# First loads in order of use on two queues, and k and q in turn, in a fused linear-attention and GEGLU kernel

## The chip, the cores and the metric

The kernel runs on one core of a Trainium2 chip. The time is device microseconds of one execution. Each kernel was timed in several executions. All runs below were classed as "fast". The profile is of one of those executions, and its span is about 1.4 us shorter than the time of the same run.

Names used below: PE is the tensor engine, PEld its weight loads, DVE the vector engine, ACT the scalar engine, SP the engine that here only issues transfers. A *pair* is the two matmuls, 512 and 128 columns wide, with which one 128-row block of x meets one 128-row piece of a weight matrix. Five pairs make k (or q) of one tile of 128 tokens.

## The reference, cut to what matters

```python
# S = 2048 tokens, D = 640, 32 heads of 20, F = 1728, bf16
qkv = x @ wqkv                                   # q, k, v
pq, pk = phi(q), phi(k)                          # phi(t) = (t + 1 if t > 0 else exp(t)) + 1e-6
kv, z = einsum(pk, v), pk.sum(tokens)
a = (einsum(pq, kv) / (einsum(pq, z) + 1e-6)) @ wo
b = (gelu(x @ w_gate) * (x @ w_up)) @ w_down
g = sigmoid((x * gate_w).sum(-1))
out = g * a + (1 - g) * b
```

The change touches only how the kernel gets started: the first loads, and the stage that computes phi(k) and phi(q) for the 16 tiles of x.

## The kernel before

A helper records every operation with the data that it reads and writes, and derives the semaphore waits from that. Each engine runs its operations in the order in which they were recorded (PE in before: `T(0)` at 3.36 us, `T(1)` at 4.65, the first pair at 5.05, `T(2)` at 5.54). The first three tiles of x (0, 1, 2) are loaded plainly and transposed on PE; the other 13 come through transposing transfers. `wk` and `wq` are the k and q columns of `wqkv`, five pieces of 128 rows each (160 KB a piece).

```python
dma_in(gw_sb[0:5, :], gate_w..., [r_gw], eng="act")
for k in range(KC):                                              # KC = 5
    dma_in(wk[:, k, :], A_wqkv[k*128:(k+1)*128, 640:1280], [r_wk[k]], eng="act")
for i in range(NXN):                                             # NXN = 3
    dma_in(x_aug[:, i, 0:640], A_x[0, i*128:(i+1)*128, :], [r_xn[i]])        # on SP
for i in range(NXN, NT):                                         # NT = 16
    load_xT(i)                                                   # transposing, on SP
# ... later loads cut ...

def T(i):        # five 128x128 transposes on PE into one bank, one DVE copy to xT
def KM(i, ks):   # pairs of k of tile i for the pieces ks of wk, into the two banks of slot(i)
def QM(i):       # five pairs of q of tile i (one more column: the gate)
def phi1(n):     # ACT: exp of the slot
def phi2(n):     # DVE: min, then max(t + 1, ...): frees the slot's banks

warm(6, 512)     # matmuls on constants, meant to get PE's clock up (e11 runs without them)
T(0); warm(2, 128); T(1); warm(2, 128)
KM(0, [0]); T(2)
# ... transpose of the gate column, its copy into wq ...
KM(1, [0])
for k in range(1, KC):
    KM(0, [k]); KM(1, [k]); KM(2, [k - 1])
KM(2, [KC - 1])
for n in range(2 * NT):          # 16 tiles of k, then 16 of q
    if n >= NT: QM(n - NT)
    elif n >= 3: KM(n, list(range(KC)))
    phi1(n); phi2(n)
    if n == 3: dma_in(wq[:, :, 0:640], ..., [r_wq], eng="act")
# ... pk^T x, FFN with geglu, normalisation, output: unchanged, cut ...
```

There are four slots of two PSUM banks each. The pairs of tile 4 go to the slot of tile 0, so they wait until DVE has finished phi of tile 0 (12.60 us in before, where they start at 12.66).

## Time and profile before

| | value | where it is read |
|---|---|---|
| time | 277.33 us, median of the first 3 runs | runs |
| span of the profiled run | 275.9 us | page |
| PE busy | 98% | page, part 1 |
| chain of waits on PE | 95% | page, part 4 |
| PE idle before the fourth piece of wk | 1.27 us | timeline |
| k of tile 3 starts / k of tile 4 starts | 11.29 / 12.66 us | timeline |

The page of before, part 1 (engine, busy us and share, number of instructions):

```profile
span 275.9 us, 4037 instructions
...
PE 269.3 (98%) x1663; PEld 139.6 (51%) x1696; DVE 138.4 (50%) x233; ACT 78.2 (28%) x132; POOL 26.0 (9%) x28
```

The timeline of before, PE only (start, duration, engine, line, operation, output and input, shape, count; in brackets the idle time just before and what ended it). L386 is the warm-up, L402 the transposes of a tile, L418 the 512-wide half of a k pair:

```profile
0.84 2.72 PE L386 MATMUL ps<-const-bfloat16-1.0 128*128 128x512 bf16 x6 [0.84 <-PEq L790]
...
3.36 0.63 PE L402 MATMUL ps<-pool 128*128 128x128 bf16 x5
...
4.65 0.45 PE L402 MATMUL ps<-pool 128*128 128x128 bf16 x5 [0.55 <-DMA pool<-in_A_x_dram]
...
5.05 0.38 PE L418 MATMUL ps<-pool 128*128 128x512 bf16 x1
...
9.38 0.39 PE L418 MATMUL ps<-pool 128*128 128x512 bf16 x1 [1.27 <-DMA pool<-in_A_wqkv_dram]
...
11.29 0.38 PE L418 MATMUL ps<-pool 128*128 128x512 bf16 x1
...
12.66 0.39 PE L418 MATMUL ps<-pool 128*128 128x512 bf16 x1
```

One sees the first transposes at 3.36 us, as soon as x tile 0 is there, the first pair at 5.05, and eight pairs later the only long idle time. A duration of 0.38 us is not the cost of a matmul: pairs follow each other every 0.27 us, and their records overlap (the first 512-wide one lasts from 5.05 to 5.43 us, the next matmul starts at 5.27). From 11.29 us on PE is dense.

What the idle PE waited for is in the view of transfers, taken over a stretch that two issues share (2.80 to 2.90 us): destination and source, queue, kind, count, KB, and us from issue to landing.

```profile
pool<-in_A_wqkv_dram ACTq DMA_DIRECT2D x1, 160.0 KB, 6.6
pool<-in_A_x_dram SPq DMA_TRANSPOSE x1, 7.6
```

The fourth piece of wk, issued at 2.75 us, landed 6.6 us later, while x tile 0, issued at 0.81, had needed 2.3. In the stretch from 5 to 6 us the same view shows why one may suspect the transposing loads (packets, bytes, rate, packets by size; then the ACT queue's own share):

```profile
DMA packets 469, 0.24 MB, mean 244 GB/s; under 512 B 343, under 2 KB 469, under 8 KB 469
...
q10 hardware_dynamic: 145, 0.16, 62.5%
```

Most packets (343 of 469) are the small ones of the transposes by then, and the rate has fallen, from 353 GB/s in the microsecond before to 244, although at least three pieces of wk are still under way on the ACT queue (q10).

### The profile page before, as it was taken

The numbers are of one execution on the slowest core, as the hardware profiler recorded it, in microseconds if no ns is written. First come the engines' busy times: TensorE is split into PE (matmuls) and PEld (weight loads), VectorE is DVE, ScalarE is ACT, GpSimd is POOL, SyncE is SP. The second block draws the span as 40 slices with busy tenths as digits, with TensorE's granted clock in tenths as the row PEclk, the third lists the DMA queues.
The fourth block names the chain that finished last, engine by engine and source line by source line (L and its number), as shares of the span: only waits on it lengthen the run. The fifth ranks groups of instructions, "written<-read, shape, count | busy, mean of one in ns | idle before, by whom it ended". The sixth has DMA issues, their size and how long they took to land.

```text
span 275.9 us, 4037 instructions
## 1 busy us (share of the span) xinstructions
PE 269.3 (98%) x1663; PEld 139.6 (51%) x1696; DVE 138.4 (50%) x233; ACT 78.2 (28%) x132; POOL 26.0 (9%) x28
## 2 busy tenths in 40 slices
PE   7899999999999999999999999999999999999997
PEld 4455555555545444444444444444555555555553
DVE  2398888610244224999999999535100122212223
ACT  1355555310432354222322223224555100000000
POOL 5000000000000400332423322000000000000000
PEclk9999999999999999999999999999999999999999
DMA  7999997002030112122121221390000011111111
GB/s 183 165 200 251 397 399 234 12 0 50 14 57 11 47 52 61 24 48 40 33 49 24 48 41 32 56 314 14 0 0 2 9 43 46 48 50 48 50 39 56
DMA packets 36400, 22.38 MB, mean 81 GB/s; under 512 B 25759, under 2 KB 34975, under 8 KB 36383
## 3 DMA queue, kind: packets, MB, share of 16 engines
q1 hardware_dynamic: 34997, 20.49, 27.6%
q10 hardware_dynamic: 1386, 1.64, 2.3%
q8 instruction: 13, 0.21, 0.4%
q14 instruction: 4, 0.03, 0.0%
HBM read 13.11 MB, written 2.62 MB: 57 GB/s over the span
## 4 chain that ended last, share of the span: by engine, by line
PE 95%; DMA 2%; issue 1%; ACTq 1%; DVE 0%
PE ps L595 41%; PE ps L738 20%; PE ps L431 6%; PE ps L701 6%; PE ps L502 6%; PE ps L418 5%; DMA pool<-in_A_wqkv_dram 2%; PE ps L504 2%; PE ps L432 2%; PE ps L702 2%; PE ps L419 2%; PE ps L570 2%; PE ps L722 1%; ACTq L330 1%; PE ps L616 1%
## 5 line engine op out<-in xcount | busy, mean ns | idle before, releaser
L595 PE MATMUL ps<-pool 128*128 128x512 bf16 x509 | 113.0, 379 | 0.6
L595 PEld LDWEIGHTS ps<-pool 128*128 128x128 bf16 x520 | 50.4, 98 | 60.0 <-issue 0.3
L738 PE MATMUL ps<-pool 128*128 128x128 bf16 (+1 forms) x407 | 56.6, 297 | 0.6 <-issue 0.2
L603 DVE TENSOR_TENSOR pool<-ps,pool 128x512 bf16<-128x512 f32 x52 | 35.7, 687 | 33.6 <-PE ps L595 30.4
L601 ACT ACTIVATE pool<-ps 128x512 f32<-128x512 f32 x52 | 31.0, 597 | 72.5 <-PE ps L595 72.1
L749 DVE SCALAR_TENSOR_TENSOR pool<-ps,pool 128x512 bf16<-128x512 f32 (+1 forms) x32 | 16.2, 547 | 63.8 <-PE ps L738 63.8
L738 PEld LDWEIGHTS ps<-pool 128*128 128x128 bf16 x416 | 31.8, 98 | 25.3 <-issue 1.1
L647 POOL TENSOR_TENSOR pool<-pool 128x640 f32<-128x640 bf16 x16 | 22.4, 1404 | 140.5 <-DMA pool<-z_row 87.4
L440 ACT ACTIVATE pool<-ps 128x640 bf16<-128x640 f32 x32 | 22.3, 703 | 23.4 <-PE ps L419 13.8
L453 DVE SCALAR_TENSOR_TENSOR pool<-ps,pool 128x640 bf16<-128x640 f32 x32 | 26.4, 824 | 2.2
L655 DVE TENSOR_TENSOR pool<-pool 128x640 bf16<-128x640 bf16 x16 | 23.0, 1440 | 0.6
L418 PE MATMUL ps<-pool 128*128 128x512 bf16 x77 | 21.6, 379 | 1.3 <-DMA pool<-in_A_wqkv_dram 1.3
L431 PE MATMUL ps<-pool 128*128 128x512 bf16 x77 | 21.4, 379 | 0.0
L701 PE MATMUL ps<-pool 128*128 128x512 bf16 x77 | 21.3, 379 | 0.0
L502 PE MATMUL ps<-pool 128*128 128x512 bf16 x76 | 21.2, 379 | 0.0
L504 PE MATMUL ps<-pool 128*128 128x129 bf16 x80 | 17.6, 220 | 0.2
L432 PE MATMUL ps<-pool 128*128 128x129 bf16 x80 | 17.6, 220 | 0.2
L702 PE MATMUL ps<-pool 128*128 128x128 bf16 x80 | 17.5, 219 | 0.2
L419 PE MATMUL ps<-pool 128*128 128x128 bf16 x80 | 17.5, 219 | 0.2
L706 ACT ACTIVATE pool<-ps,pool 128x640 f32<-128x640 f32 x16 | 12.7, 793 | 9.2 <-PE ps L702 9.2
L450 DVE TENSOR_SCALAR pool<-pool 128x640 bf16<-128x640 bf16 x32 | 10.4, 325 | 7.9 <-ACT pool L440 6.3
L418 PEld LDWEIGHTS ps<-pool 128*128 128x128 bf16 x80 | 7.8, 98 | 10.8 <-DMA pool<-in_A_wqkv_dram 1.6
(51 smaller groups left out, 128.9 us busy)
## 6 DMA issues: line engine op xcount, KB each, us to landing
out_dram<-pool SPq DMA_DIRECT2D x15, 160.0 KB, 1.8
pool<-in_B_w_gate_dram SPq DMA_DIRECT2D x1, 2080.0 KB, 13.9
pool<-in_B_w_up_dram SPq DMA_DIRECT2D x1, 2080.0 KB, 18.5
pool<-in_A_x_dram SPq DMA_DIRECT2D x1, 1280.0 KB, 7.7
pool<-in_B_w_down_dram SPq DMA_DIRECT2D x1, 1120.0 KB, 6.0
pool<-in_A_wo_dram SPq DMA_DIRECT2D x6, 160.0 KB, 8.8
pool<-in_B_w_down_dram SPq DMA_DIRECT2D x1, 960.0 KB, 8.4
pool<-in_A_wqkv_dram ACTq DMA_DIRECT2D x5, 160.0 KB, 4.4
```

The costliest lines, as they stand in the source:

```text
L418: e.matmul(ps[:, b0, :], lhs, wk[:, k, 0:512], start=(k == 0), stop=(k == KC - 1))
L419: last = e.matmul(ps[:, b1, 0:128], lhs, wk[:, k, 512:640], start=(k == 0), stop=(k == KC - 1))
L431: e.matmul(ps[:, b0, :], lhs, wq[:, k, 0:512], start=(k == 0), stop=(k == KC - 1))
L432: last = e.matmul(ps[:, b1, 0:129], lhs, wq[:, k, 512:641], start=(k == 0), stop=(k == KC - 1))
L453: P.op("dve", lambda e: e.scalar_tensor_tensor(dst, ps_flat[:, b0 * 512:b0 * 512 + 640], 1.0 + EPS, e_buf[m], ALU.add, ALU.max), reads=[ba ...
L502: e.matmul(ps[:, bs[n], :], lhs, x_aug[:, i, 0:512], start=(i == 0), stop=(i == NT - 1))
L504: last = e.matmul(ps[:, bt, n * 129:(n + 1) * 129], lhs, x_aug[:, i, 512:641], start=(i == 0 and n == 0), stop=(i == NT - 1), skip_group_c ...
L595: last = e.matmul(ps[:, b, :], w[:, k, fc * 128:(fc + 1) * 128], xT[:, k, j * 512:(j + 1) * 512], start=(k == 0), stop=(k == KC - 1))
L601: P.op("act", lambda e: e.activation(ge[n], ps[:, gb, :], ACT.Gelu_apprx_tanh), reads=[bank[gb]], writes=[r_ge[n]])
L603: P.op("dve", lambda e: e.tensor_tensor(hT[fc][:, j * 512:(j + 1) * 512], ps[:, ub, :], ge[n], ALU.mult), reads=[bank[ub], r_ge[n]], write ...
L701: e.matmul(ps[:, b0, :], lhs, w2[:, m, 0:512], start=(m == 0), stop=(m == KC - 1))
L738: last = e.matmul(dst, lhs, wd[:, fc, c0:c0 + cn], start=False, stop=(fc == NFC - 2), skip_group_check=True)
```

## The change

The intent: the first loads in the order of their use, spread over both queues (x0, wk1, x2, wk3 on SP; wk0, x1, wk2, wk4 on ACT); the transposing loads not before wk1 has landed; wq moved from ACT into the stream of transposing loads; k of seven tiles first, then q and k in turn, so that later transposed tiles are needed at half the pace; and tile 0's first block transposed and copied alone, so that the first pair can start early.

```diff
+KLEAD = 7
-dma_in(gw_sb[0:5, :], gate_w..., [r_gw], eng="act")
-for k in range(KC):
-    dma_in(wk[:, k, :], ..., [r_wk[k]], eng="act")
-for i in range(NXN):
-    dma_in(x_aug[:, i, 0:640], ..., [r_xn[i]])
+load_x(0, "sp");  load_wk(0, "act")
+load_wk(1, "sp"); load_x(1, "act")
+load_x(2, "sp");  load_wk(2, "act")
+load_wk(3, "sp"); load_wk(4, "act")
+dma_in(gw_sb[0:5, :], gate_w..., [r_gw], eng="act")
 for i in range(NXN, NT):
-    load_xT(i)
+    if i == KLEAD:
+        dma_in(wq[:, :, 0:640], ..., r_wq)
+    load_xT(i, after=([r_wk[1]] if i == NXN else ()))
 ...
+seq = [("k", i) for i in range(KLEAD)] + [("q", 0)]
+for i in range(KLEAD, NT):
+    seq += [("q", i - KLEAD + 1), ("k", i)]
+seq += [("q", i) for i in range(NT - KLEAD + 1, NT)]
 ...
 warm(6, 512)
-T(0); warm(2, 128); T(1); warm(2, 128); KM(0, [0]); T(2); <gate column>; KM(1, [0])
-for k in range(1, KC):
-    KM(0, [k]); KM(1, [k]); KM(2, [k - 1])
-KM(2, [KC - 1])
+T(0, [0], 7); T(0, [1, 2, 3, 4], 6)
+KM(0, [0]); T(1, [0, 1, 2, 3, 4], 7); KM(0, [1]); warm(2, 128)
+KM(1, [0]); KM(1, [1]); T(2, [0, 1, 2, 3, 4], 6)
+KM(0, [2]); KM(1, [2]); KM(2, [0]); KM(2, [1]); KM(2, [2]); gate_col()
+for k in range(3, KC):
+    for n in range(3):
+        KM(n, [k])
```

(Cut: bookkeeping of which data a step reads, and `phi1`, `phi2`, `QM` looking up their tile in `seq`.)

More of the change, by code (lines that the diff above doesn't have):

```diff
@@ L299, in bass_gated_mix__linear_attn_block__geglu_ffn__prompt_kernel @@
             r_xT = [P.sb("xT%d" % i, R_XT, R_XT + KC * S) for i in range(NT)]
+            r_x0a = P.sb("x0a", R_XT, R_XT + 128)
             r_wk = [P.sb("wk%d" % k, R_WK + k * 640, R_WK + (k + 1) * 640) for k in range(KC)]
-            r_wq = P.sb("wq", R_WQ, R_WQ + KC * XW)
+            r_wq = [P.sb("wq%d" % k, R_WQ + k * XW, R_WQ + k * XW + 640) for k in range(KC)]
             r_gcol = P.sb("gcol", R_WQ, R_WQ + KC * XW)
@@ L331, in dma_in, with load_x, load_wk @@
                      reads=reads, writes=writes, dma=new_dma_key())
+            def load_x(i, eng):
+                dma_in(x_aug[:, i, 0:640], A_x[0, i * 128:(i + 1) * 128, :], [r_xn[i]], eng=eng)
+            def load_wk(k, eng):
+                dma_in(wk[:, k, :], A_wqkv[k * 128:(k + 1) * 128, 640:1280], [r_wk[k]], eng=eng)
+            load_x(0, "sp")
+            load_wk(0, "act")
+            load_wk(1, "sp")
+            load_x(1, "act")
+            load_x(2, "sp")
+            load_wk(2, "act")
+            load_wk(3, "sp")
+            load_wk(4, "act")
             dma_in(gw_sb[0:5, :], gate_w.rearrange("(k p) -> k p", p=128), [r_gw], eng="act")
-            for k in range(KC):
-                dma_in(wk[:, k, :], A_wqkv[k * 128:(k + 1) * 128, 640:1280], [r_wk[k]], eng="act")
-            for i in range(NXN):
-                dma_in(x_aug[:, i, 0:640], A_x[0, i * 128:(i + 1) * 128, :], [r_xn[i]])
             def load_xT(i, after=()):
@@ L345, in bass_gated_mix__linear_attn_block__geglu_ffn__prompt_kernel @@
             for i in range(NXN, NT):
-                load_xT(i)
+                if i == KLEAD:
+                    dma_in(wq[:, :, 0:640], A_wqkv[:, 0:640].rearrange("(k p) w -> p k w", p=128), r_wq)
+                load_xT(i, after=([r_wk[1]] if i == NXN else ()))
             dma_in(x_aug[:, NXN:8, 0:640],
@@ L394, in slot, with T @@
                 return SLOTS[n] if n < 3 else SLOTS[n % 4]
-            def T(i):
-                tb = 6 + i % 2
+            def T(i, ks, tb):
                 def fn(e):
                     last = None
-                    for k in range(KC):
-                        last = e.transpose(psb[:, tb, k * 128:(k + 1) * 128],
+                    for n, k in enumerate(ks):
+                        last = e.transpose(psb[:, tb, n * 128:(n + 1) * 128],
                                            x_aug[:, i, k * 128:(k + 1) * 128], ident)
@@ L406, in T, with KM @@
                 P.op("dve", lambda e: e.tensor_copy(
-                    xT[:, :, i * 128:(i + 1) * 128],
-                    psb[:, tb, 0:640].rearrange("p (k s) -> p k s", k=KC)),
-                    reads=[bank[tb]], writes=[r_xT[i]])
-            def KM(i, ks):
-                b0, b1 = slot(i)
+                    xT[:, ks[0]:ks[-1] + 1, i * 128:(i + 1) * 128],
+                    psb[:, tb, 0:len(ks) * 128].rearrange("p (k s) -> p k s", k=len(ks))),
+                    reads=[bank[tb]], writes=[r_x0a if i == 0 and ks[0] == 0 else r_xT[i]])
+            seq = [("k", i) for i in range(KLEAD)] + [("q", 0)]
+            for i in range(KLEAD, NT):
+                seq += [("q", i - KLEAD + 1), ("k", i)]
+            seq += [("q", i) for i in range(NT - KLEAD + 1, NT)]
+            def KM(n, ks):
+                i = seq[n][1]
+                b0, b1 = slot(n)
                 def fn(e):
@@ L421, in fn, with QM @@
                     return last
-                P.op("pe", fn, reads=[r_xT[i]] + [r_wk[k] for k in ks], writes=[bank[b0], bank[b1]])
-            def QM(i):
-                b0, b1 = slot(NT + i)
+                P.op("pe", fn, reads=[r_x0a if i == 0 and ks == [0] else r_xT[i]] + [r_wk[k] for k in ks],
+                     writes=[bank[b0], bank[b1]])
+            def QM(n):
+                i = seq[n][1]
+                b0, b1 = slot(n)
                 def fn(e):
@@ L434, in fn @@
                     return last
-                P.op("pe", fn, reads=[r_xT[i], r_wq, r_gcol], writes=[bank[b0], bank[b1]])
+                P.op("pe", fn, reads=[r_xT[i], r_gcol] + r_wq, writes=[bank[b0], bank[b1]])
             def phi1(n):
@@ L441, in phi1 @@
                      reads=[bank[b0], bank[b1]], writes=[r_e[m]])
-                if n >= NT:
-                    i = n - NT
+                kind, i = seq[n]
+                if kind == "q":
                     P.op("act", lambda e: e.activation(eg[:, i:i + 1], ps[:, b1, 128:129], ACT.Tanh, scale=0.5),
@@ L451, in phi2 @@
                      reads=[r_e[m]], writes=[r_e[m]])
-                dst, r_dst = (pk[n], r_pk[n]) if n < NT else (pq[n - NT], r_pq[n - NT])
+                kind, i = seq[n]
+                dst, r_dst = (pk[i], r_pk[i]) if kind == "k" else (pq[i], r_pq[i])
                 P.op("dve", lambda e: e.scalar_tensor_tensor(
@@ L455, in phi2, with gate_col @@
                     reads=[bank[b0], bank[b1], r_e[m]], writes=[r_dst])
-            warm(6, 512)
-            T(0)
-            warm(2, 128)
-            T(1)
-            warm(2, 128)
-            KM(0, [0])
-            T(2)
-            P.op("pe", lambda e: e.transpose(psb[:, 7, 0:5], gw_sb[0:5, :], ident[0:5, 0:5]),
-                 reads=[r_gw, r_ident], writes=[bank[7]])
-            P.op("dve", lambda e: e.tensor_copy(wq[:, :, 640:641],
-                                                psb[:, 7, 0:5].rearrange("p (k o) -> p k o", o=1)),
-                 reads=[bank[7]], writes=[r_gcol])
-            KM(1, [0])
-            for k in range(1, KC):
-                KM(0, [k])
-                KM(1, [k])
-                KM(2, [k - 1])
-            KM(2, [KC - 1])
+            def gate_col():
+                P.op("pe", lambda e: e.transpose(psb[:, 7, 0:5], gw_sb[0:5, :], ident[0:5, 0:5]),
+                     reads=[r_gw, r_ident], writes=[bank[7]])
+                P.op("dve", lambda e: e.tensor_copy(wq[:, :, 640:641],
+                                                    psb[:, 7, 0:5].rearrange("p (k o) -> p k o", o=1)),
+                     reads=[bank[7]], writes=[r_gcol])
+            warm(6, 512)
+            T(0, [0], 7)
+            T(0, [1, 2, 3, 4], 6)
+            KM(0, [0])
+            T(1, [0, 1, 2, 3, 4], 7)
+            KM(0, [1])
+            warm(2, 128)
+            KM(1, [0])
+            KM(1, [1])
+            T(2, [0, 1, 2, 3, 4], 6)
+            KM(0, [2])
+            KM(1, [2])
+            KM(2, [0])
+            KM(2, [1])
+            KM(2, [2])
+            gate_col()
+            for k in range(3, KC):
+                for n in range(3):
+                    KM(n, [k])
             for n in range(2 * NT):
-                if n >= NT:
-                    QM(n - NT)
+                if seq[n][0] == "q":
+                    QM(n)
                 elif n >= 3:
@@ L481, in bass_gated_mix__linear_attn_block__geglu_ffn__prompt_kernel @@
                 phi2(n)
-                if n == 3:
-                    dma_in(wq[:, :, 0:640], A_wqkv[:, 0:640].rearrange("(k p) w -> p k w", p=128), [r_wq],
-                           eng="act")
                 if n == 6:
```

## The prediction

> **What bounds the kernel.** The tensor engine. The page of before shows PE busy 98% of a 275.9 us span, and the chain of waits is 95% PE. The table of stretches shows PE busy 9.9 of 10 us from 12 us to the end of the k/q stage, granted clock 1.0 throughout. So nothing after about 12 us can be shortened by this change: it moves loads and reorders the same 32 k/q tiles, which cost 5 pairs of matmuls at 0.27 us, 1.36 us each. ACT (0.70 us) and DVE (0.33 + 0.82 us) per tile stay below that. Only the start can be won.
>
> **The start in the timeline.** x tile 0 lands at 3.1 us; the first k pair starts at 5.05 after five transposes, a 0.49 us copy and small warm-up matmuls, with 0.55 us of PE idle. Eight pairs have run by 8.11, then PE idles 1.27 us, until 9.38, for the fourth piece of wk, which was issued at 2.75 and landed 6.6 us later, sharing the DMA engines with thirteen transposing x loads that were issued from 2.2 us on. The seven remaining pairs end at 11.28, where k of tile 3 starts. The same work packed from first data is about 4.1 us of pairs plus 1 us of transposes.
>
> **What the change does.**
> 1. x0 and wk0 go first on two queues, then wk1/x1, x2/wk2, wk3/wk4; transposing loads wait until wk1 has landed. Eight loads of 160 KB are 1.31 MB. With both queues plain the trace moved about 300 to 350 GB/s (3 to 5 us), so I estimate 1 us per couple: landings near 3.3, 4.3, 5.3 and 6.3 us. [...] I credit the gain to order and to the transposes kept out, not to added bandwidth. Issues here cost 0.37 to 0.45 us.
> 2. Tile 0's first block is transposed and copied alone: the first pair at about 3.9 instead of 5.05 us.
> 3. From these: T2 done near 6.1, seven pairs by 7.5, gate column, last eight pairs without a stall, k of tile 3 near 9.2 instead of 11.28. Gain 2.1 us.
> 4. Costs: transposing loads begin near 4.4 instead of 2.2 us. Alone they landed 3.0 to 4.0 us after issue, one every 1.28 us: tile 3 near 8.2, tile 6 near 12.5, each before its use (9.2, 13.4). wq sits between tiles 6 and 7: issued near 9.5, landing (5.5 us before, beside transposes) 14 to 15 us, against first use near 14.8. This is the tight spot; up to 0.7 us may be lost.
> 5. After that k and q alternate, so each transposed tile is needed every 2.7 us, and their supply has slack. No work is added later; the stages after k/q should only shift.
>
> **Prediction.** 275.3 us (0.993), range 274.4 to 276.6. Faster by over 2% would need 5.5 us, more than the whole startup idle: chance 0.01. Within 2%: 0.98. Slower: 0.01.
>
> **What would show it.** Timeline: first k pair near 3.9 us, no wait of PE on wk over 0.3 us, tile 3's k near 9.2; wait of q0 on wq under 0.7 us; PE busy total the same within 1 us; later stages starting about 2 us earlier with equal lengths.
>
> **What would make it wrong.** x0 arriving later because wk0 shares its engines (each 0.3 us costs as much); wk3/wk4 caught by the transposes again; tile 3 or wq late, which would hand the gain back at once, since PE has no slack afterwards.

That the second queue would add no bandwidth was the assumption (measured afterwards, from 2 to 3 us: 201 GB/s from one queue in before, 207 from two in the changed kernel). The forecast's sum: landings 1 us apart, the first pair at 3.9, k of tile 3 at 9.2, a gain of 2.1 us.

## The result, and the profile after

| | before | after |
|---|---|---|
| time, median of 6 runs (lowest to highest) | 277.39 us (277.02 to 277.52) | 276.73 us (276.53 to 278.38) |
| ratio | | 0.9988, 95% interval 0.9964 to 1.0012 |
| span of the profiled run | 275.9 us | 275.2 us |
| first transposes start | 3.36 us | 4.17 us |
| first pair starts | 5.05 us | 4.72 us |
| k of tile 3 starts | 11.29 us | 10.36 us |
| k of tile 4 starts | 12.66 us | 12.00 us |
| span minus start of tile 4 | 263.2 us | 263.2 us |

A ratio is the mean time of one kernel's fast runs over that of the other's fast runs of the same rounds, so it is not quite the ratio of the medians. Here one run of 278.38 us among five of 276.5 to 277.0 pulls the mean up. The interval contains 1, so these runs alone do not show that the changed kernel is faster; what follows reads two profiles, and the experiments below bear it out.

The last row says where the whole difference between the two profiles lies: after k of tile 4 has started, both take the same 263.2 us. The second half of the change, k and q in turn, moved nothing; all of their difference, 12.66 - 12.00 = 0.66 us, was won in the first 12 us. Forecast had been 2.1 us.

The page after, part 1. (The higher busy time than before is not work: records of matmuls are missing from the trace of before, which has 1663 for 1696 weight loads, against 1694 for 1694 after.)

```profile
span 275.2 us, 4067 instructions
...
PE 271.3 (99%) x1694; PEld 139.3 (51%) x1694; DVE 138.8 (50%) x234; ACT 78.3 (28%) x132; POOL 26.1 (9%) x28
```

The timeline after, PE, the lines that answer to those of before (L401 warm-up, L415 transposes, L438 k pair):

```profile
0.84 2.72 PE L401 MATMUL ps<-const-bfloat16-1.0 128*128 128x512 bf16 x6 [0.84 <-PEq L818]
4.17 0.45 PE L415 MATMUL ps<-pool 128*128 128x128 bf16 x5 [0.61 <-DMA pool<-in_A_x_dram]
4.72 0.39 PE L438 MATMUL ps<-pool 128*128 128x512 bf16 x1
...
6.04 0.39 PE L438 MATMUL ps<-pool 128*128 128x512 bf16 x1 [0.20 <-DVE pool L419]
...
10.36 0.38 PE L438 MATMUL ps<-pool 128*128 128x512 bf16 x1
...
12.00 0.39 PE L438 MATMUL ps<-pool 128*128 128x512 bf16 x1
```

The long idle time before 9.38 us is gone, as intended. But the first transposes now start 0.81 us later than before, the second tile's first pair waits for a copy (L419), and tile 4, which needs 1.36 us after tile 3 when nothing is in the way, starts 1.64 us after it.

The transfers after: the two first loads (issued at 0.80 and 0.81 us), in the columns used above.

```profile
pool<-in_A_wqkv_dram ACTq DMA_DIRECT2D x1, 160.0 KB, 3.1
pool<-in_A_x_dram SPq DMA_DIRECT2D x1, 160.0 KB, 3.3
```

x0 needed 3.3 us instead of 2.3. (In the other profiles whose two first loads are these it needed 2.9 to 3.3 us, so a single landing time has a scatter of about 0.4 us.) wk0 landed at 3.9 us; in before, where it was issued at 1.40, at 4.8. And the stretch from 5 to 6 us, which is now plain packets (48 of 303 are under 512 B, where before had 343 of 469):

```profile
DMA packets 303, 0.33 MB, mean 328 GB/s; under 512 B 48, under 2 KB 303, under 8 KB 303
...
q10 hardware_dynamic: 141, 0.15, 42.1%
```

The chain of waits after, in order of time (start, us, what), shows the links of the start:

```profile
0.81 3.32 DMA pool<-in_A_x_dram
4.17 0.24 PE ps L415
4.44 0.24 DVE pool L419
4.72 0.39 PE ps L438
...
5.49 0.50 DVE pool L419
6.04 0.39 PE ps L438
...
10.02 0.71 ACT pool L462
10.75 0.34 DVE pool L472
11.12 0.84 DVE pool L476
12.00 0.39 PE ps L438
```

The last four lines are phi of tile 0: its exp starts only at 10.02, when its last pair has ended, and its bank is free at 12.00. That is the 0.28 us between tiles 3 and 4.

### The profile page after: what moved, and what is told of

Same layout as the page of the kernel before. It is cut to its first block, busy times and chain, and to the rows that moved or that the text cites. A ratio compares the mean times of both kernels' runs of the same rounds, so it can differ in the third digit from the quotient of the medians.

```text
span 275.2 us, 4067 instructions
## 1 busy us (share of the span) xinstructions
PE 271.3 (99%) x1694; PEld 139.3 (51%) x1694; DVE 138.8 (50%) x234; ACT 78.3 (28%) x132; POOL 26.1 (9%) x28
## 4 chain that ended last, share of the span: by engine, by line
PE 96%; DMA 1%; DVE 1%; ACT 0%; issue 0%
PE ps L623 41%; PE ps L766 20%; PE ps L530 6%; PE ps L729 6%; PE ps L453 6%; PE ps L438 6%; PE ps L454 2%; PE ps L532 2%; PE ps L730 2%; PE ps L598 2%; PE ps L439 1%; DMA pool<-in_A_x_dram 1%; PE ps L750 1%; PE ps L644 1%; PE ps L660 1%; DVE pool L777 0%
## 5 line engine op out<-in xcount | busy, mean ns | idle before, releaser
L623 PE MATMUL ps<-pool 128*128 128x512 bf16 x520 | 113.7, 379 | 0.0
L766 PE MATMUL ps<-pool 128*128 128x512 bf16 (+1 forms) x416 | 57.2, 299 | 0.0
L438 PE MATMUL ps<-pool 128*128 128x512 bf16 x80 | 23.5, 380 | 0.5 <-DVE pool L419 0.2
L453 PE MATMUL ps<-pool 128*128 128x512 bf16 x80 | 22.9, 379 | 0.0
L530 PE MATMUL ps<-pool 128*128 128x512 bf16 x80 | 21.9, 379 | 0.0
L729 PE MATMUL ps<-pool 128*128 128x512 bf16 x80 | 21.8, 379 | 0.0
L677 DVE TENSOR_REDUCE pool<-pool 128x32 f32<-128x640 f32 x16 | 13.0, 810 | 0.0
L438 PEld LDWEIGHTS ps<-pool 128*128 128x128 bf16 x80 | 7.8, 98 | 10.1 <-DVE pool L419 1.0
```

Source lines behind the costliest of these rows:

```text
L438: e.matmul(ps[:, b0, :], lhs, wk[:, k, 0:512], start=(k == 0), stop=(k == KC - 1))
L453: e.matmul(ps[:, b0, :], lhs, wq[:, k, 0:512], start=(k == 0), stop=(k == KC - 1))
L530: e.matmul(ps[:, bs[n], :], lhs, x_aug[:, i, 0:512], start=(i == 0), stop=(i == NT - 1))
L623: last = e.matmul(ps[:, b, :], w[:, k, fc * 128:(fc + 1) * 128], xT[:, k, j * 512:(j + 1) * 512], start=(k == 0), stop=(k == KC - 1))
L729: e.matmul(ps[:, b0, :], lhs, w2[:, m, 0:512], start=(m == 0), stop=(m == KC - 1))
L766: last = e.matmul(dst, lhs, wd[:, fc, c0:c0 + cn], start=False, stop=(fc == NFC - 2), skip_group_check=True)
```

## The experiments

Theory: the whole difference, and the whole shortfall, lies before k of tile 4. Of the 2.1 us, 0.8 went to x0, which shares the DMA engines with wk0 now (from 3 to 4 us the packets of SP's queue took 48.6% of the 16 engines' time, those of ACT's 61.5%); the rest to copies that PE waits for and to the order of the pairs. Rivals: k and q in turn gives something back (e1); the hold of the transposing loads costs or gains (e2); x0 was late for another reason (e3). While these ran, PE's clock came up as another rival, which the later runs test. Every kernel gave the correct result. Ratios are against the kernel before, which ran beside each group (medians 277.35 to 277.57 us; in the group of e9 to e12 its runs went from 276.54 to 279.56, which widens those intervals: the kernel before has an occasional slow run too). By the verdict at 2% every kernel of the table counts as "same"; differences of a few tenths of a microsecond are read from intervals, from groups of runs and from profiles.

| kernel | median us (lowest to highest) | ratio, 95% interval |
|---|---|---|
| e1 all k, then all q | 276.71 (276.35 to 276.98) | 0.9980 (0.9968 to 0.9993) |
| e2 no hold | 276.49 (276.39 to 277.07) | 0.9977 (0.9964 to 0.9990) |
| e3 x0 alone first | 277.20 (277.13 to 278.26) | 1.0010 (0.9993 to 1.0028) |
| e4 tile 0's pairs first | 276.36 (276.28 to 276.50) | 0.9968 (0.9956 to 0.9981) |
| e5 seven warm-ups | 276.65 (276.40 to 277.06) | 0.9978 (0.9965 to 0.9992) |
| e6 = e4 + seven warm-ups | 276.26 (275.92 to 276.56) | 0.9962 (0.9948 to 0.9975) |
| e7 = e4, x0 and wk0 in halves | 278.74 (278.00 to 279.72) | 1.0054 (1.0035 to 1.0074) |
| e8 before, new loads only | 279.70 (276.71 to 280.33) | 1.0061 (1.0019 to 1.0103) |
| e9 = e6 without hold | 276.34 (276.10 to 276.56) | 0.9956 (0.9925 to 0.9986) |
| e10 = e8, idle gaps filled | 276.74 (276.42 to 277.17) | 0.9974 (0.9945 to 1.0002) |
| e11 no warm-up | 277.90 (277.44 to 278.36) | 1.0014 (0.9985 to 1.0042) |
| e12 tile 0 transposed whole | 278.28 (276.97 to 278.55) | 1.0015 (0.9982 to 1.0047) |
| e13 = e7, idle gaps filled | 277.29 (277.06 to 279.03) | 1.0011 (0.9986 to 1.0035) |
| e14 = e12, idle gap filled | 277.14 (276.75 to 277.60) | 0.9995 (0.9974 to 1.0015) |

### e1: the alternation undone

```diff
-seq = [("k", i) for i in range(KLEAD)] + [("q", 0)] ...
+seq = [("k", i) for i in range(NT)] + [("q", i) for i in range(NT)]
```

> The changed kernel, with the alternation of k and q undone (all k, then all q); loads and prologue kept. Theory S (the whole difference to before, and the whole shortfall, lies in the first 12 us): the same time as the changed kernel, 276.7 us within 0.2, as PE is dense after 12 us there and each transposed tile still lands before its use. Rival R (the reordering of k and q hands back some of the gain, through ACT's extra activation or the wait for wq): 0.5 us or more faster than the changed kernel.

Measured: 276.71 us, against 276.73. In its profile tile 4 starts at 12.09 us and the span is 275.3: again 263.2 us from there to the end. The alternation neither costs nor gains anything that these runs can show; before did not need the slack that it creates.

### e2: the transposing loads not held

```diff
-load_xT(i, after=([r_wk[1]] if i == NXN else ()))
+load_xT(i)
```

> The changed kernel without the wait of the transposing loads on wk1. If keeping them out is what removed the wait on wk, then x2, wk3 and wk4 land 1 to 3 us later, PE waits 1 us or more on a load before the k of tile 3, and the time returns to before's 277.4 or above. If order alone did it, the time stays at 276.7 and the landings at about 6.7 to 7.2 us.

Measured: 276.49 us, no slower. The first transposing load is issued at 2.6 instead of 4.84 us, yet x2, wk3 and wk4 land at about 6.2, 7.0 and 7.2 us; with the hold it was 6.6, 7.2 and 6.8 (and 6.0, 6.8 and 7.05 in e1, which has the hold too, so these differences are scatter). So the hold is not what keeps the transposes off the plain loads. The likely reason, an estimate that no run tests by itself, is the queues: on SP the transposes stand behind x2 and wk3, and the ACT queue is through at about the same time. The packets of the two traces fit: in the changed kernel the first packet of a transposing load starts on SP's queue at 6.21 us, when all but 8 of its 512 plain packets have started, and the last plain one on ACT's at 6.16. In before, SP had only three tiles in front of them (last packet at 5.04 us, first of the transposes at 5.08), while ACT still had two to three pieces of wk to bring, and brought 0.16, 0.09 and 0.09 MB a microsecond beside the transposes from 5 to 8 us. How the DMA engines divide their time between the two queues was not shown.

### e3: x0 with the DMA engines to itself

```diff
+dma_in(gw_sb[0:5, :], gate_w..., [r_gw], eng="act")      # first on ACT, as before
 load_x(0, "sp"); load_wk(0, "act")
 ...
-dma_in(gw_sb[0:5, :], gate_w..., [r_gw], eng="act")
```

> The changed kernel with the small gate load first on the ACT queue, as before, so that wk0 is issued about 0.6 us later and x0 has the DMA engines to itself. Theory S1 (x0 landed at 4.1 and not 3.1 us because wk0 shared its engines): x0 lands at 3.1 to 3.3 us again and the first transpose starts by 3.6. Whether it pays depends on wk0: it landed at 4.8 us in before; then the first k pair stays near 4.7 and the time at 276.7 within 0.2. Rival S2 (x0 was late for another reason, such as HBM): x0 still lands near 4.1.

Measured: 277.20 us, slower than expected by 0.3. The timeline of PE in e3:

```profile
3.35 0.74 PE L415 MATMUL ps<-pool 128*128 128x128 bf16 x5
4.49 0.55 PE L438 MATMUL ps<-pool 128*128 128x512 bf16 x1 [0.40 <-DMA pool<-in_A_wqkv_dram]
...
5.57 0.45 PE L415 MATMUL ps<-pool 128*128 128x128 bf16 x5 [0.48 <-DMA pool<-in_A_x_dram]
```

x0 landed 2.3 us after its issue, at 3.1, and the transposes started at 3.35, as in before: so wk0, which e3 issues 0.6 us later on the other queue, is what delayed x0 in the changed kernel. But nothing is won by letting x0 go first, because the first pair needs wk0 too, and then x1 comes later (5.5 us). Two loads of 160 KB are needed for the first pair, whoever goes first. That is where the forecast of 3.9 us failed.

### e4: each tile's pairs as far as they have landed, tile 0 finished first

```diff
-KM(0,[1]); warm(2,128); KM(1,[0]); KM(1,[1]); T(2); KM(0,[2]); KM(1,[2]); KM(2,[0..2]); gate_col(); <k = 3, 4: KM(0), KM(1), KM(2)>
+KM(0,[1]); KM(0,[2]); warm(2,128); KM(1,[0]); KM(1,[1]); KM(1,[2]); T(2); gate_col(); KM(0,[3]); KM(0,[4]); KM(1,[3]); KM(1,[4]); <KM(2) k = 0..4>
```

> The changed kernel with the 15 k pieces of tiles 0 to 2 in another order: each tile's pieces as far as they have landed, tile 0 finished first, the gate column in the gap behind the transposes of tile 2. Theory S3 (part of the gain was lost to PE waiting on two copies of transposed tiles, 0.2 us each, on the gate column, 0.25, and on DVE before the k of tile 4, 0.34, because tile 0 ends too late): the k of tile 3 starts near 9.7 instead of 10.36 us, that of tile 4 near 11.1 instead of 12.0, and the time is 275.8, within 0.3. Rival: the loads set the start and PE only waits elsewhere: 276.6 or more.

Measured: 276.36 us, so the direction is right and the size is less than half of what was expected. In the profile tile 3 starts at 10.40, not earlier than in the changed kernel, but tile 4 follows at 11.76 without a wait, instead of at 12.00. The wait for DVE is shown; the gain at tile 3 is missing. A likely cause is in the first lines of the timeline:

```profile
4.08 0.71 PE L415 MATMUL ps<-pool 128*128 128x128 bf16 x5 [0.53 <-DMA pool<-in_A_x_dram]
4.69 0.61 PE L438 MATMUL ps<-pool 128*128 128x512 bf16 x1
...
5.20 0.74 PE L415 MATMUL ps<-pool 128*128 128x128 bf16 x5
```

The same transposes that took 0.45 us in the changed kernel's profile took 0.71 and 0.74, the matmul 0.61 instead of 0.39: PE ran at half speed until about 6.0 us. A second cause would have cost the same: wk2 landed only at 6.21 us in this profile, and the pair that needs it started at 6.25. In e9, below, half speed alone sufficed: wk2 landed at 5.71 there, and that pair started at 6.25 too.

### e5 and e6: seven warm-up matmuls

```diff
-warm(6, 512)
+warm(7, 512)
```

> The changed kernel with seven instead of six warm-up matmuls, so that PE stays busy to about 4.0 us, until x0 lands. In four profiles of kernels with these loads the first transposes took 0.71 us and the first pair's 512-column matmul 0.61 instead of 0.45 and 0.39: PE ran at half speed until about 5.4 us after idling from 3.56. Theory H (the idle gap before x0 keeps the PE clock low and costs the start 0.3 to 0.6 us): T1 and its pair run at full speed, KM of tile 4 starts by 11.8, and the time falls to 276.2 to 276.5. Rival (the clock depends on luck, or what follows absorbs it): 276.7 or more.

> The kernel e4 (order of the k pieces, tile 0 first) with seven warm-up matmuls. e4 gained 0.3 to 0.4 us on the changed kernel although its PE ran at half speed until about 5.5. If theory H holds, and order and clock add: 275.8 to 276.1. If the wait for wk2 at 6.1 to 6.3 us bounds it in either case: 276.3, as e4.

Measured: e5 276.65 us, no gain; in its profile PE was busy with no gap worth noting from 0.84 to 6 us and still at half speed until 6.3 (the 512-wide matmul at 5.71 took 0.64 us, that at 6.50 0.39). So the single gap before x0 is not what decides when the clock comes up in that run. Full speed came 3 us after the start of the warm-up in before and 5.5 us after it in e5, and in e7, below, full, half and full speed follow each other at 3.47, 6.88 and 10.30 us in the clock records, two steps of 3.4 us. What sets these moments was not shown. They differ between kernels with the same order on PE: the first transposes took 0.45 us at 4.12 in e6 and 0.72 at 4.07 in e9, which stayed at half speed until 6.7. So the author takes it to be partly luck how early the clock comes up in a run. Before and the changed kernel happen to have profiles in which it came early (first clock record at 3.74 and 3.86 us), which makes those two comparable; in e1, e2, e4, e5 and e9 it came at 5.4 to 6.6 us.

e6 had 276.26 us, the number that was expected if the wait for wk2 bounds it, but not for that reason: wk2 landed at 5.51 us in its profile, and another wait took its place. In this profile PE was at full speed from the first transposes on (0.45 us at 4.12), tile 3 started at 9.78 and tile 4 at 11.14, 0.86 us earlier than in the changed kernel, although the first pair started at 4.67, hardly earlier than there (4.72). This is one start whose clock came up early, not the median. Tiles 3 and 4, then the first q:

```profile
9.78 0.38 PE L438 MATMUL ps<-pool 128*128 128x512 bf16 x1
...
11.14 0.38 PE L438 MATMUL ps<-pool 128*128 128x512 bf16 x1
...
15.16 0.22 PE L439 MATMUL ps<-pool 128*128 128x128 bf16 x1
15.98 0.38 PE L453 MATMUL ps<-pool 128*128 128x512 bf16 x1 [0.60 <-DVE pool L476]
```

The profile names DVE, but DVE had freed that slot at 13.3 us; what landed just then is wq, issued at 10.2 us and 5.6 us under way, at 15.8. The tight spot that the prediction named is real, and appears once the start is faster.

### e7 and e13: x0 and wk0 cut into halves; the gaps filled

```diff
-load_x(0, "sp"); load_wk(0, "act")
+x0 rows 0:64 on SP, rows 64:128 on ACT; then wk0 rows 64:128 on SP, rows 0:64 on ACT
```

> The kernel e4 with x0 and wk0 each cut into two halves of 64 rows, one half of x0 first on each queue, then one half of wk0; six warm-up matmuls. Theory S1 (x0 is late because wk0's bytes share its engines): x0 lands near 3.3, wk0 near 4.0, the first pair starts near 4.1 to 4.3 instead of 4.7, PE is never idle before it, and the time is 275.7 to 276.0. Rival (landing is set by a fixed latency or the slow first microsecond): x0 lands at 3.6 or later and the time stays at 276.2 or above.

Measured: 278.74 us, the opposite of what was expected. x0 did land at 3.4 us, but one half of wk0 only at 4.5: two more issues stood on the queues (0.56 us for the first half on each, against 0.40 for a whole load in the changed kernel), and x1, wk2 and wk4 came 1.1 to 1.6 us later than in the changed kernel. PE had three idle gaps of 0.7 us, and after the third it was at half speed:

```profile
4.61 0.38 PE L444 MATMUL ps<-pool 128*128 128x512 bf16 x1 [0.68 <-DMA pool<-in_A_wqkv_dram]
...
5.74 0.45 PE L421 MATMUL ps<-pool 128*128 128x128 bf16 x5 [0.69 <-DMA pool<-in_A_x_dram]
...
7.17 0.61 PE L444 MATMUL ps<-pool 128*128 128x512 bf16 x1 [0.71 <-DMA pool<-in_A_wqkv_dram]
```

Here the view by stretches shows the clock as well (stretch, its length, busy us of PE, PEld, DVE, ACT and POOL with counts, then the granted TensorE clock, DMA share, GB/s):

```profile
5.00:6.00 1.00, 0.30 (x6) 0.27 (x6) 0.00 (x0) 0.80 (x1) 0.00 (x0) 1.00 0.91 312
...
7.00:8.00 1.00, 0.83 (x5) 0.56 (x6) 0.00 (x0) 0.00 (x0) 0.00 (x0) 0.50 1.32 114
```

The granted clock is 0.50 from 6.88 to 10.30 us. The mean clock that is listed for each run tells of this drop too: it is 0.994 in the four runs of e7 that took 278.6 to 279.7 us, and 1.000 in the two that took 278.0 and 278.1.

e13 puts warm-up matmuls into the three gaps and changes nothing else:

```diff
 T(0, [0], 7); T(0, [1, 2, 3, 4], 6)
+warm(6, 128)
 KM(0, [0])
+warm(8, 128)
 T(1, ...); KM(0, [1])
+warm(8, 128)
 KM(0, [2])
```

> e7 (x0 and wk0 in halves) with small warm-up matmuls in PE's three idle gaps of 0.7 us (6, 8 and 8 of 128 columns). Theory H (idle gaps keep or put PE at half speed): no pair is slow after 7.2 us, where e7's were at half speed to about 10, and the time is 276.2 to 277.0 instead of 278.7; no run over 278. Rival (the later landings of the halves alone made e7 slow): 278 or more remains.

Measured: 277.29 us, 1.45 less than e7, with no slow pair after 5.4 us in its profile (the transposes at 6.16 us were the last slow ones). Five runs lie at 277.1 to 277.6, above the expected 276.2 to 277.0, and one at 279.0, which the theory had excluded; no profile shows what happened in that one. Cutting the loads into halves of the partitions gained nothing here: 277.29 against 276.36 for e4, the same order without halves (and without the filling matmuls).

### e8 and e10: the new loads alone; the gaps filled

e8 is the kernel before with the eight first loads of the change; PE's order and wq as before. e10 fills its gaps:

```diff
-warm(6, 512); T(0); warm(2, 128); T(1); warm(2, 128); KM(0, [0]); T(2); <gate column>
+warm(7, 512); T(0); warm(4, 128); T(1); warm(4, 128); KM(0, [0]); warm(4, 128); T(2)
 ...
 KM(2, [KC - 1])
+<gate column>
```

> The kernel before with the new order of loads on the two queues alone (no hold of the transposes, wq still from ACT, old PE order). Theory S: PE's wait on the fourth piece of wk (1.27 us) is gone, but x0 lands at 3.7 to 4.1 instead of 3.1 and the first pair at 5.5 to 5.8, x2 at 6.2 to 6.6: KM of tile 4 starts at 12.0 to 12.4 and the time is 276.7 to 277.1. If the changed kernel's PE order is what gains and not the loads, it is 277.3.

> e8 (before with the new order of loads alone), with PE's idle gaps filled: seven warm-ups, four small warm-up matmuls after each transpose, and the gate column moved behind the k pieces, where it waits for nothing. In e8's profile PE ran pairs at 0.53 instead of 0.27 us until 12.9; four of its six runs took 279.3 to 280.3 us and two 276.7 to 276.9. Theory H (idle gaps in the first 8 us keep the clock at half, depending on where they fall): no pair is slow after 7 us and all runs lie at 276.4 to 277.2. Rival (the slow start is luck, or the loads are at fault): runs near 280 remain.

Measured: e8 has two groups of runs, two as expected (276.7 and 276.9), and four at 279.3 to 280.3. The profile is of a slow one (span 278.8 us). No wait for wk is left, as expected; but PE waited 0.71 us for the gate vector, which now comes last, and ran at half speed:

```profile
7.70 0.18 PE L474 MATMUL ps<-pool 5*128 5x5 bf16 x1 [0.71 <-DMA pool<-in_gate_w_dram]
7.81 0.61 PE L428 MATMUL ps<-pool 128*128 128x512 bf16 x1
...
9.39 0.63 PE L428 MATMUL ps<-pool 128*128 128x512 bf16 x1
9.81 0.32 PE L429 MATMUL ps<-pool 128*128 128x128 bf16 x1
9.92 0.64 PE L428 MATMUL ps<-pool 128*128 128x512 bf16 x1
```

Pairs follow every 0.53 us instead of 0.27, up to 13.1 us: from 7.81 to 13.1 that is ten pairs, 2.6 us too long. The view by stretches says 1.00 throughout for the granted clock here, although in e7 it showed the drop. The clock records in the packed trace, which no view prints, explain this: e8's first one starts at 13.20 us (3.74 in before, 3.86 in the changed kernel) and nothing is recorded before it, so the half speed of the start shows only in durations and spacing. e10, 276.74 us, has no run above 277.2, and no slow pair after 6.3 us. Its edits do three things at once (one more long warm-up, more small ones, the gate moved), so it speaks for the gaps together as the cause, and does not tell which one.

### e11 and e12: no warm-up; tile 0 transposed whole; e14: e12's gap filled

```diff
# e11
-warm(6, 512)
# e12
-T(0, [0], 7); T(0, [1, 2, 3, 4], 6)
+T(0, [0, 1, 2, 3, 4], 6)
# e14 = e12 and
-warm(6, 512); T(0, [0, 1, 2, 3, 4], 6)
+warm(7, 512); T(0, [0, 1, 2, 3, 4], 6); warm(6, 128)
```

> The changed kernel without the six warm-up matmuls at its start. Theory H: PE starts at half speed at about 4.1 us[...]; some 8 to 15 of the first pairs cost 0.53 instead of 0.27 us, and the time is 278 to 280.5. Rival (PE's clock at the start hardly matters because loads bound it): within 0.4 of 276.7.

> The changed kernel with tile 0 transposed and copied in one piece again. The prediction gave this split the first pair at 3.9 instead of 5.05 us. If it carries gain: first pair 0.25 us later, 276.9 to 277.0. If the next waits (x1 and the copy of tile 1) absorb it: within 0.15 of the changed kernel, 276.7.

> e12 (tile 0 transposed in one piece) with seven warm-ups and six small ones while the copy of tile 0 runs. e12's six runs were two at 277.0 and four at 278.3 to 278.6; its profile, of a 277.0 run, shows PE idle 0.40 and 0.59 us around the first transposes, but full speed. Theory H (in its slow runs PE was at half speed because of those gaps): all runs at 276.8 to 277.3. Rival (another cause): runs at 278.3 and more remain.

Measured: e11 277.90 us, 1.2 more than the changed kernel and just under the expected range; full speed came at 9.36 us, 5.6 us after PE's first work, and seven recorded pairs were slow (0.61 to 0.63 us for the 512-wide matmul). e12 had two runs at 277.0 and four at 278.3 to 278.6. The profile, of a run at 276.97, shows full speed by the first pair (0.39 us for its 512-wide matmul), PE idle for 0.40 us before the transposes and 0.59 before the first pair, and the first pair at 5.11; its span is 275.5 us, 0.3 more than the changed kernel's. This much of the split's worth was expected. The four slow runs were not. e14 has none of them, 276.75 to 277.60 us (a little wider than expected). By this reading the split of tile 0 is worth more than its copy's time: it also closes a gap. That half speed was what made e12's slow runs slow is inferred from e14, not seen.

Taken together, the kernels with gaps had 6 (e7), 4 (e8) and 4 (e12) runs of 278 us and more out of six, the filled ones 1 (e13), 0 (e10) and 0 (e14). The filled ones ran later and on other chips than those that they fill, so a difference between chips in how often the clock comes up late was not excluded within one group of runs.

### A version that beats both kernels

e4, e6 and e9 have ratios of 0.9956 to 0.9968 to the kernel before, with intervals wholly below 1. Against the changed kernel, which ran in other rounds, there are only the medians: 0.4 to 0.5 us less. e9 was meant to take e6's wait for wq away:

```diff
# e9 = e6 and
-load_xT(i, after=([r_wk[1]] if i == NXN else ()))
+load_xT(i)
```

> e6 (tile 0's pieces first, seven warm-ups) without the hold of the transposing loads. In e6's profile PE waited 0.60 us at 15.4 before the first q, whose wq was issued at 10.2 and landed 5.6 us later. Without the hold wq was issued at 8.0 in e2. Theory W (once the start is faster, the late wq takes back what it won): the wait is gone and the time falls by up to 0.6 us from e6's 276.26, to 275.6 to 275.9. Rival (the wait was for DVE, which the profile names, or the earlier transposes delay the plain loads): the wait stays, 276.2 or more.

Measured: 276.34 us, not the expected 275.6 to 275.9. wq was issued at 8.0 us, landed at 13.6, and the first q started at 16.01 without any wait; that part is shown. But the profiled run, 276.56 us, was at half speed until about 6.7 us (0.63 us for the 512-wide matmul at 5.71, 0.38 at 6.83), so its tile 4 started at 11.94 and it reached the first q later anyway. What the wait is worth in the median stays open. From e6's start (tile 4 at 11.14) and the 263.2 us that follow in most profiles, a span of about 274.3 us is an estimate of what the two together would give in a run whose clock comes up early. No run showed it; the nearest are two runs of e6 with spans of 274.5 us.

## Why the prediction was wrong

That the time would stay within 2% came true, and was nearly certain, as the prediction itself says that more would need 5.5 us. The gain did not come true: 0.66 us instead of 2.1. The step that failed is step 1, when the first loads land, with step 2, which rests on it; step 3 also left out a wait. Point by point:

1. *PE bounds the kernel and only the start can be won*: right. Span minus start of tile 4 is 263.2 us in before, after, e1, e2, e3 and e4.
2. *"landings near 3.3, 4.3, 5.3 and 6.3 us"* (step 1): wrong from the first couple on. x0 landed at 4.1, wk1 and x1 at 4.8 and 4.6, x2 at 6.6, wk3 at 7.2. The sum left out that the transfer starts slowly: from 2 to 3 us the trace after moved only 207 GB/s over both queues together, as before did with one queue (201), and 387 from 3 to 4. The two first loads needed about 2 us from their first packets (1.83 and 2.01) to their landings (3.9 and 4.1), not 1. e3 shows that wk0 beside it is what delays x0.
3. *"the first pair at about 3.9 instead of 5.05 us"* (step 2): 4.72. From the landing of x0 to the first pair it was 0.6 us, as forecast (3.3 to 3.9); the landing was 0.8 late. This is 0.8 of the missing 1.4 us. With the same two first loads the first pair started at 4.37 to 4.72 us in the profiles of e1, e2, e11 and after. Neither e3 (4.49, x0 first) nor e7 (4.61, halves) lies outside this scatter, so neither rearrangement made it earlier.
4. *"k of tile 3 near 9.2 instead of 11.28"* (step 3): 10.36. Beyond the 0.8 above, 0.3 went to waits of about 0.2 us each for the copies of tiles 1 and 2 and around the gate column, of which the forecast had allowed for a part; the late x2 held its transposes by less than 0.1 us. (The step counts seven and eight pairs. Nine stand before the gate column and six after it, and only with these do its times add up: 7.5 + 6 x 0.27 = 9.1.)
5. Left out of the prediction: the pairs run piece by piece over three tiles, so tile 0 ends third from last; phi of tile 0 then frees its slot 0.28 us after PE could have used it. e4 takes this wait away. In before, the same chain from tile 0's last pair just fitted, as one pair more stood between.
   Together: 0.8 + 0.3 + 0.3 = 1.4 us. This is the account of one profile against the forecast, not three measured effects. e6 warns against taking it as such: its first pair is as late, and yet its tile 4 starts 0.86 us earlier, with another order of the pairs and one more warm-up matmul. So more than the last two terms could be won without any earlier landing of x0. How the shortfall divides in the median of the runs stays open.
6. *Hold of the transposes*: the credit was misplaced. e2 without it is as fast; the new loads as a whole take the wait for wk away (e8). Their order and their spread over two queues were not tested apart.
7. *wq as the tight spot*: no wait in the changed kernel, since its start was slow; 0.6 us in e6.
8. *"k and q alternate ... supply has slack"*: right, but e1 shows that nothing needed it.
9. *"granted clock 1.0 throughout"* was said of the time from 12 us on, and holds there. PE's speed in the first microseconds was not asked about: the warm-up's matmuls are 0.43 us apart in every profile that has them, at half speed (in the first pair of before the next matmul starts 0.22 us after a 512-wide one). In the changed kernel's profile full speed came by 4.17 us, so this is not where the 1.4 us went there; but its run of 278.38 us has the size of the slow runs of e12, and may be one. That is a guess.

## What to carry to other kernels

Here the first matmul needs two loads, and putting them on two queues shared the start between them: x0 came 0.6 to 1.0 us later than in before, wk0, issued 0.6 us sooner, came 0.9 us earlier, and the first pair gained 0.33 us in the profile of after. Cost the start by bytes until the *last* one needed, with the transfer rate of the first microsecond as the trace shows it. After removing one wait in a start-up, write down the next one behind it (here copies, then a slot's release, then wq) before promising the whole gap. Keep PE free of idle gaps in the first microseconds, since runs of a kernel with gaps of 0.3 to 0.7 us (e8) took up to 3.6 us more than its best one, and judge the clock at the start by the spacing of equal matmuls (pairs 0.53 instead of 0.27 us apart in e8, where the clock read 1.00).

## What the traces show of the clock and the transfers

- In e7, with three idle gaps of 0.7 us, PE was at half speed from 6.88 us, within the third, to 10.30; in e8, with one of 0.71 us after smaller ones, PE ran at half speed until 13.1 us. Filling them (e13, e10) took 1.45 us off the median of e7 and 3 us off that of e8. From what length on a gap matters was not shown.
- The granted clock read 1.00 while pairs ran at 0.53 instead of 0.27 us, before the first clock record at 13.20 us (e8), but read 0.50 in a later drop (e7).
- x0, whose issue took from 0.81 to 1.21 us, had its first packet at 1.82 us in before and 2.01 in after: 0.6 to 0.8 us after the end of the issue, and 1.0 to 1.2 after its start. It landed 2.3 us after the start of its issue alone and 2.9 to 3.3 beside another load of 160 KB.
- From 2 to 3 us one queue moved 201 GB/s (before) and two moved 207 (after), but which loads stood on which queue and in which order decided a wait of 1.27 us (before against e8).
- The issue of a transposing load of 128 x 640 took 1.28 us (before, median of 13), and the loads followed each other no faster.
